# A gated mix of linear attention and a Fourier layer: the first four tiles of k' computed chunk by chunk for both column halves in eight banks, and the stores of x's rest rows moved behind the last loads of their stage

## The chip, the core and the metric

The kernel runs on one core of a Trainium2 chip. The metric is the device time of one execution in microseconds, and the figure compared is the median over several executions. A profile, taken of one more execution, records every instruction of the five engines (TensorE or PE, VectorE or DVE, ScalarE or ACT, GpSimd or POOL, SyncE or SP) and every DMA packet.

## What is computed

Two branches read the same `x` (2048 rows, 576 columns) and are mixed by a gate per row.

```
g = sigmoid(sum(x * gate_w))                          # one number per row
q, k, v = split(x @ wqkv)                             # 32 heads of 18 columns
phi(t) = where(t > 0, t + 1, exp(t)) + 1e-6
kv = phi(k)^T v;  z = sum over rows of phi(k)         # per head
a = (phi(q) kv / (phi(q) z + 1e-6)) @ wo
b = Re(DFT_seq(DFT_hidden(x)))                        # four dense DFT matrices
out = g * a + (1 - g) * b
```

All is float32. The products run on TensorE in float32r, a faster form that keeps fewer bits: an operand is split into a high part `hi` and a low part `lo = raw - hi`, and a product is `hi*hi + hi*lo + lo*hi`, three matmuls.

## The kernel before

**Stages.** In the order of time: k' = phi(x @ wk) for 16 tiles of 128 rows (lines 440 to 579, to 68 us of the profile); x^T k' for the attention's state, with one product `kv_step` per chunk of 128 columns of x (lines 582 to 690, 68 to 135 us); q' = phi(x @ wq) and the gate (from line 693, 130 to 200 us), the attention's output, and then the two DFT passes, which take the larger part of the time (lines 845 to 1205). A memory area, `arena`, is laid out by hand: names ending in `_AT` are offsets, and areas are used again from stage to stage. The framework orders instructions that touch the same bytes with semaphores.

**k'.** The contraction of 576 is cut into four chunks of 128 and a rest of 64, held as one more chunk of 128 with the rest twice (`_rows`, line 1209), so that one matmul with `hi` and one with `lo` of x do its work. The 576 columns of wk make two halves (`h`) of 288, each fitting one PSUM bank (there are eight). One half of one tile is `4 x 3 + 2 = 14` matmuls of 128x288, 28 a tile (`steps`, line 269). Tiles 4 to 15 run one after another, half by half (`k_half`, line 447). `feature` (line 338) turns a finished bank into phi: two ACT instructions (lines 340, 341) and one on DVE (342) that frees the bank; `k_split` (457) then makes the high and low parts `pk` of a whole tile. `k_split`s wait in the list `pending`.

**The first four tiles** (lines 464 to 531) go by chunks, so that matmuls can start when the first chunk of wk and x has landed: for half 0, chunk after chunk, the passes over the four tiles in four banks; then half 1 in the other four banks. `Wide.load` (294) issues the pieces of one half of wk: chunks 0, 1 and 2-3 of half 0, then the rest, then half 1 in two pieces of two chunks and its rest. Between them `load_first` (468) issues the chunks of `xf`, the first four tiles of x: chunk 0 in two parts of two tiles, chunk 1, chunks 2-3, chunk 4. Parts of `xf` go to ACT's queue, all else to SP's. As a chunk lands, ACT makes its `hi` (`hi_of`, line 172) and DVE its `lo` (`lo_of`, 182); in `Wide.split` (313) for wk, written out in the loop for x. Then come ACT's and DVE's work in the order of the program, since `pace()` (line 489) turns the framework's own ordering off for these two; SP's queue is in program order throughout. PE's order is the framework's at this stage.

**The features of the first tiles** run in two groups, half 0's four (line 525) after both halves' matmuls have been issued, then `split_next` twice (526, 527), which splits x tiles 4 and 5, then half 1's four, with two `k_split`s between them. In the loop over tiles 4 to 15 (557) each turn runs one half, splits an x tile two ahead, does a part of a `Left` (below), runs the other half and the pending `k_split`s, and issues the load of a tile four ahead (`load_next`, 253). Four slots hold tiles of x (`LAY_Q['xs']`, 78).

**DMA issue.** A DMA signals its end on one of eight semaphores in turn; the ninth DMA waits for the first one's landing, and so on.

**Left and the rest rows.** `Left` (349) prepares, beside the attention, combinations of x's transpose for the DFT stage: loads on POOL's queue, four DVE additions, `hi` and `lo`, stores. The last of them, `Left(NP)`, holds the rows left over from the contraction's 128s. It lies at `ACC_AT`, over `acc[0]` to `acc[6]`, loaded at step 6 of the second stage when k' no longer needs them there. It ends with six stores of 448 KB to `xrest` on SP's queue (lines 385 to 387), issued as soon as its parts are done, in the middle of that stage's loads: `xg_load` (539, the pieces `craw` of x), `load_pair` (600, wv and wo) . q' writes `acc` again (line 703, `feature`). `xrest` is read from line 889 on, in the DFT stage.

Of the kernel before, what the change touches and what calls it, by code (L numbers as in the profile page):

```python
# [8 lines left out]
F = mybir.dt.float32  # L9
R = mybir.dt.float32r  # L10
# [43 lines left out]
class Ring:  # L54
# [5 lines left out]
    def next(self):  # L60
        self.n += 1
        return self.at[(self.n - 1) % len(self.at)]
# [7 lines left out]
SLOT_AT, SLOT = ACC_AT + NT * D * 4 + 256, 7 * BS * P * 4  # L70
# [61 lines left out]
def kernel(  # L132
# [18 lines left out]
    nc = tc.nc  # L151
# [17 lines left out]
    def bank():  # L169
        return psum.tile([P, 512], F, tag="bank", name="bank")  # L170

    def hi_of(dst, src, bias=0.0):
        return nc.scalar.activation(dst, src, AF.Copy, bias=bias)  # L173


    pending, paced = [], ExitStack()
# [5 lines left out]
    def lo_of(dst, src, hi):  # L182
        nc.vector.tensor_tensor(out=dst, in0=src, in1=hi, op=ALU.subtract)  # L183
# [21 lines left out]
    def half(h):  # L205
        return slice(h * HALF, (h + 1) * HALF)
# [78 lines left out]
    rest_ring = Ring(CONST_AT + 3584, 1184, 2)  # L285

    class Wide:
# [6 lines left out]
        def load(self, h, pieces=(KC,), queues=None, also=lambda k: None):  # L294
# [15 lines left out]
            also(len(los))  # L310
            queues[-1].dma_start(out=rest, in_=self.src[:, KC, cols])

        def split(self, h, n=1, lo_of=lo_of):
# [12 lines left out]
            lo_of(hi[64:, KC], rest[64:], hi[64:, KC])  # L326
            yield
# [19 lines left out]
    xrest_of = xrest.rearrange("(g q j r) n -> g j r q n", g=2, q=4, j=3)  # L347

    class Left:
# [18 lines left out]
        def make(self):  # L368

            r, c = self.f[:, :, 1], self.c  # L370
            add(r[:, 0], r[:, 1], r[:, 6])
            add(r[:, 4], r[:, 2], r[:, 6], ALU.subtract)
            yield
            add(r[:, 3], r[:, 0], r[:, 2], ALU.subtract)
            add(r[:, 6], r[:, 5], r[:, 3], ALU.subtract)
            yield
            hi_of(c[:, :4, 0], r[:, :4])
            hi_of(c[:, 4:, 0], r[:, 4:])
            yield
            for fs in (slice(0, 4), slice(4, 7)):  # L380
                lo_of(c[:, fs, 1], r[:, fs], c[:, fs, 0])
                if self.k < NP:
                    nc.gpsimd.dma_start(out=xforms[self.k][:, fs], in_=c.bitcast(F)[:, fs])
                yield
            for j in range(0 if self.k < NP else 6):
                k, g = j // 2, j % 2
                nc.sync.dma_start(out=xrest_of[g, k], in_=self.plain.bitcast(F)[:, g, k // 2])

    lefts = []

    def left_part():
        while lefts:
# [50 lines left out]
    wkt = Wide(wk, dict(hi=(0, WH), lo=(2 * WH, 2 * WH + WL)), K_AT)  # L443

    done = []
# [19 lines left out]
    first, cuts = [], ((0, 1), (1, 1), (2, 2), (4, 1))  # L465
    ab = [slice(k * FT // 2 * P, (k + 1) * FT // 2 * P) for k in range(2)]

    def load_first(k):
        nonlocal first_b
        a, n = cuts[k]  # L470
        o = C_AT + a * 2 * FT * P * 4
        hi, raw, lo = (at(o + i * n * FT * P * 4, [P, n, FT * P], d, "xs")
                       for i, d in ((0, R), (1, F), (1, R)))
        src = xf[a:a + n].rearrange("c p n -> p c n")
        if k == 0:
            first_b = raw[:, :, ab[1]], src[:, :, ab[1]]
            raw_a, src = raw[:, :, ab[0]], src[:, :, ab[0]]
        elif k == 1:
# [4 lines left out]
    first_b = None  # L483
    wkt.load(0, (1, 1, 2), also=load_first)
    wkt.load(1, (2, 2))
    order += list(range(FT, NT)) + list(range(NT))
    for _ in range(3):
        load_next()
    pace()
    for h in range(2):  # L490
        ps = [bank()[:, :HALF] for _ in range(FT)]
        parts = wkt.split(h, KC)
        for c, (raw, hi, lo) in enumerate(first):
            passes = [(hi, c), (lo, c), (hi, 5 + c)][:3 if c < KC else 2]
            tiles = [range(FT)] * len(passes)
            if h == 0 and c == 0:
                a, b = ab
                nc.vector.tensor_copy(out=hi[:, a], in_=raw[:, a])
                lo_of(lo[:, a], raw[:, a], hi[:, a])
                next(parts)  # L500
                done.append(hi_of(hi[:, b], raw[:, b]))
                lo_of(lo[:, b], raw[:, b], hi[:, b])
                two = range(FT // 2), range(FT // 2, FT)
                passes = [(hi, c), (lo, c), (hi, c), (hi, 5 + c), (lo, c)]
                tiles = [two[0], two[0], two[1], range(FT), two[1]]
            elif h == 0 and c == 1:
                next(parts)
                done.append(hi_of(hi, raw))
                lo_of(lo, raw, hi)
                passes = [passes[k] for k in (0, 2, 1)]  # L510
            else:
                if h == 0:
                    done.append(hi_of(hi, raw))
                    lo_of(lo, raw, hi)
                next(parts)
            for n, (x, j) in enumerate(passes):
                for i in tiles[n]:
                    nc.tensor.matmul(ps[i], x[:, i * P:(i + 1) * P], wkt.row(h, j),  # L518
                                     start=(c == 0 and n == (0 if h or i < 2 else 2)),
                                     stop=(c == KC and n == 1))  # L520
        if h == 0:
            banks = ps
            lefts.append(Left(2, SLOT_AT + 15104, done[-1]).make())
    for i in range(FT):
        k_feature(i, 0, banks[i])
    split_next()
    split_next()
    for i in range(FT):
        k_feature(i, 1, ps[i])
        if i < 2:  # L530
            pending.pop(0)()

    WV_AT = C_AT + 4 * 2 * CU * P * 4
# [23 lines left out]
    for i in range(FT, NT):  # L557
        xs = split.pop(0)
        k_half(i, 0, xs)
        if i < NT - 2:  # L560
            split_next()
        left_part()
        if i >= NT - 2:
            xg_next()
        held = pending[:]
        pending.clear()
        k_half(i, 1, xs)
        for f in held:
            f()
        if 8 <= i < 12:  # L570
            xg_load()
        if i < NT - 1:
            load_next()
        if i == FT:
            load_next()
        for k, j in ((3, 4), (4, 9), (5, 13)):
            if i == j:
                lefts.append(Left(k, SLOT_AT + 15104 + k % 2 * 14336, done[-1]).make())
# [56 lines left out]
    for c in range(5):  # L635
        ps = [bank(), bank()]
        passes = FULL if c < KC else FULL[:2]
        for q in range(NCU):
            t = xg_split.pop(0)
            for k in range(CU):  # L640
                s = q * CU + k
                for n, (a, b) in enumerate(passes):
                    for h in range(2):
                        nc.tensor.matmul(ps[h][:, :HALF], t[:, a, k], pk[s][:, b, half(h)],  # L644
                                         start=(s == 0 and n == 0),
                                         stop=(s == NT - 1 and n == len(passes) - 1))
# [162 lines left out]
    def m_row(h, j):  # L809
        return mhi[:, j, half(h)] if j <= KC else mlo[:, j - 5, half(h)]  # L810

    wr_forms, wr_pieces = right(wr, wr_rest, ((0, T_AT + 60416), (1, T_AT + 76544),
                                              (2, T_AT + 60416)))
    xs_ring.at[3] = T_AT + 105664
# [310 lines left out]
    for i in range(NT):  # L1125
# [3 lines left out]
        for h in range(2):  # L1129
            ps = bank()  # L1130
# [164 lines left out]
```

## Time and profile before

| | |
|---|---|
| median of 3 executions | 729.3 us (728.0 to 729.98) |
| the profiled execution, its own time | 731.39 us |
| its span, first to last instruction | 729.7 us |
| DVE busy | 600.8 us (82%) |
| ACT busy | 335.4 us (46%) |
| POOL busy | 57.0 us (8%) |
| moved by DMA | 158.82 MB, mean 218 GB/s |
| share of the chain of work that ended last, PE | 96% |
| the same, DMA | 2% (line 309's wk 1.0%, wv 0.9%) |

How to read it: the span is what the trace covers, and the execution's own time adds what lies around it, 1.7 us here. "Busy" is a sum over instructions of one engine. The chain of work that ended last goes back from the last instruction to what released it, again and again, so a cause on it is one that the end of the kernel waited for. Where PE is busy without a break, the chain runs along PE. Times in the timeline are microseconds from the span's start; a row can merge several instructions of one form (x24 is 24 of them), and the bracket at its end gives the engine's idle time before the row and what ended it. In the table of stretches (windows) each engine has its busy time, then come the granted TensorE clock (1.00 is full speed), the share of time that the DMA engines worked, and GB/s.

### The profile page before, as it was taken

To read this page: it belongs to the slowest core of one execution; us is meant where nothing else is said; L and a number is where in the kernel's file an instruction comes from. 1 tells how busy PE (TensorE), PEld (TensorE's weight loads), DVE (VectorE), ACT (ScalarE), POOL (GpSimd) and SP (SyncE) were. 2 spreads that over 40 slices of the span, in tenths; PEclk is the share of its full clock that TensorE was granted. 3 is DMA by queue.
4 is the path that set the end of the run, shared out by engine and by line. 5 is a ranking of instruction groups with operands and counts; after the bars stand their busy time and mean duration, and the time that the engine had idled before them with its cause. 6 is when DMAs were issued, how large, how long until landed. Compare 5 with 4: busy or idle time off the path is not lost.

```text
span 729.7 us, 13873 instructions
## 1 busy us (share of the span) xinstructions
PE 721.5 (99%) x5444; PEld 720.0 (99%) x5444; DVE 600.8 (82%) x995; ACT 335.4 (46%) x522; POOL 57.0 (8%) x98
## 2 busy tenths in 40 slices
PE   8999999999999999999999999999999999999998
PEld 8999999999999999999999999999999999999997
DVE  4788885688999948989999989867889987788884
ACT  5898444678744544534343333322535333232231
POOL 1011210042022220000000010000000000000000
PEclk9999999999999999999999999999999999999999
DMA  7277699367558989853466576889964444444440
GB/s 254 70 247 247 249 328 340 98 189 234 189 169 295 335 304 374 279 185 119 153 217 228 186 234 210 282 282 392 391 235 146 156 150 147 152 144 157 152 152 33
DMA packets 54356, 158.82 MB, mean 218 GB/s; under 512 B 6420, under 2 KB 11092, under 8 KB 53268
## 3 DMA queue, kind: packets, MB, share of 16 engines
q1 hardware_dynamic: 45044, 118.90, 47.6%
q0 software_dynamic: 8960, 38.65, 14.4%
q8 instruction: 43, 0.70, 0.4%
q10 hardware_dynamic: 288, 0.39, 0.1%
q14 instruction: 21, 0.17, 0.1%
HBM read 115.05 MB, written 41.39 MB: 214 GB/s over the span
## 4 chain that ended last, share of the span: by engine, by line
PE 96%; DMA 2%; DVE 1%; SPq 0%; issue 0%; ACT 0%; DVEq 0%; ACTq 0%
PE bank L1067 48%; PE bank L203 23%; PE bank L912 14%; PE bank L644 7%; PE bank L518 2%; PE bank L747 1%; DMA wraw<-in_wk_dram 1%; DMA wraw<-in_wv_dram 1%; PE bank L626 1%; DVE row L1083 0%; PE bank L629 0%; DVE ys L193 0%; SPq L309 0%; ACT plain L173 0%; DVE wd L183 0%
## 5 line engine op out<-in xcount | busy, mean ns | idle before, releaser
L1067 PE MATMUL bank<-fh,c 128*128 128x288 f32 x1792 | 354.7, 294 | 0.0
L1067 PEld LDWEIGHTS bank<-fh,c 128*128 128x128 f32 x1792 | 286.7, 188 | 0.0
L1067 PE MATMUL bank<-fl,c 128*128 128x288 f32 x896 | 263.6, 294 | 0.0
L173 ACT ACTIVATE c<-craw 128x1792 fp32r<-128x1792 f32 (+1 forms) x84 | 121.5, 1448 | 187.5 <-DVE craw L193 164.6
L1067 PEld LDWEIGHTS bank<-fl,c 128*128 128x128 f32 x896 | 168.7, 188 | 0.0
L183 DVE TENSOR_TENSOR c<-craw,c 128x1792 fp32r<-128x1792 f32 (+4 forms) x86 | 142.0, 1653 | 6.6 <-ACT c L173 6.5
L193 DVE TENSOR_TENSOR craw<-craw 128x256 f32<-128x256 f32 (+1 forms) x192 | 98.3, 512 | 21.7 <-DMA craw<-in_ci_dram 11.9
L203 PE MATMUL bank<-wd,xs 128*128 128x288 f32 (+1 forms) x784 | 106.1, 296 | 0.0
L203 PEld LDWEIGHTS bank<-wd,xs 128*128 128x128 f32 x784 | 104.6, 188 | 0.1
L912 PE MATMUL bank<-wf,xf 128*128 128x288 f32 x588 | 91.1, 295 | 0.0
L912 PEld LDWEIGHTS bank<-wf,xf 128*128 128x128 f32 x588 | 83.4, 189 | 0.0
L203 PE MATMUL bank<-mw,qs 128*128 128x288 f32 x448 | 63.2, 297 | 0.0
L644 PE MATMUL bank<-pk,c 128*128 128x288 f32 x448 | 60.9, 296 | 1.1 <-DVE c L183 1.1
L644 PEld LDWEIGHTS bank<-pk,c 128*128 128x128 f32 x448 | 59.8, 189 | 1.3 <-DVE c L183 1.3
L203 PEld LDWEIGHTS bank<-mw,qs 128*128 128x128 f32 x448 | 59.9, 188 | 0.2 <-DVE qs L183 0.2
L342 DVE SCALAR_TENSOR_TENSOR acc<-bank,e 128x288 f32<-128x288 f32 x64 | 28.4, 454 | 17.7 <-ACT e L341 17.6
L193 DVE TENSOR_TENSOR ys<-bank,ys 128x288 f32<-128x288 f32 x63 | 28.8, 457 | 16.4 <-PE bank L1067 13.4
L183 DVE TENSOR_TENSOR fl<-fl,fh 128x864 fp32r<-128x864 f32 (+1 forms) x32 | 34.7, 1093 | 6.5 <-ACT fh L173 5.3
L173 ACT ACTIVATE fh<-fl 128x864 fp32r<-128x864 f32 (+1 forms) x32 | 29.8, 949 | 16.6 <-DVE fl L193 16.6
L912 PE MATMUL bank<-wf,xr 96*128 96x288 f32 x112 | 33.3, 298 | 0.0
L1132 ACT ACTIVATE acc<-bank,gate 128x288 f32<-128x288 f32 x32 | 16.0, 501 | 35.1 <-PE bank L203 34.8
L193 DVE TENSOR_TENSOR ys<-ys,bank 128x288 f32<-128x288 f32 x47 | 21.2, 450 | 13.0 <-PE bank L1067 12.4
(107 smaller groups left out, 668.0 us busy)
## 6 DMA issues: line engine op xcount, KB each, us to landing
xf<-xm SPq DMA_DIRECT2D x42, 512.0 KB, 6.7
craw<-in_cr_dram SPq DMA_DIRECT2D x32, 512.0 KB, 4.1
craw<-in_ci_dram SPq DMA_DIRECT2D x32, 512.0 KB, 3.5
xraw<-in_xa_dram SPq DMA_DIRECT2D x28, 320.0 KB, 3.0
xm<-xb POOLq DMA_DIRECT2D x8, 1024.0 KB, 6.6
wf<-wm SPq DMA_DIRECT2D x14, 576.0 KB, 5.9
xr<-xr SPq DMA_DIRECT2D x14, 448.0 KB, 8.8
xm<-xb POOLq DMA_DIRECT2D x8, 768.0 KB, 6.2
```

The source lines that it names most:

```text
L173: return nc.scalar.activation(dst, src, AF.Copy, bias=bias)
L183: nc.vector.tensor_tensor(out=dst, in0=src, in1=hi, op=ALU.subtract)
L193: nc.vector.tensor_tensor(out=dst, in0=a, in1=b, op=op)
L203: nc.tensor.matmul(ps, a, b, start=(n == 0), stop=(n == len(pairs) - 1))
L342: nc.vector.scalar_tensor_tensor(dst, ps, 0.0, e, op0=ALU.max, op1=ALU.add)
L518: nc.tensor.matmul(ps[i], x[:, i * P:(i + 1) * P], wkt.row(h, j), start=(c == 0 and n == (0 if h or i < 2 else 2)), stop=(c == KC and n == 1))
L626: nc.tensor.matmul(kv_of(g), wvt[c][:, 0, gs], gts[c][:, :, gs], start=(c == 0 and g % 2 == 0), stop=(c == 4), skip_group_check=True)
L644: nc.tensor.matmul(ps[h][:, :HALF], t[:, a, k], pk[s][:, b, half(h)], start=(s == 0 and n == 0), stop=(s == NT - 1 and n == len(passes) - 1))
L747: nc.tensor.transpose(banks[c // KC][:, (c % KC) * P:(c % KC + 1) * P], a, ident)
L912: nc.tensor.matmul(ps, a, b, start=(start and n == 0), stop=(n == len(ops) - 1), skip_group_check=True)
L1067: nc.tensor.matmul(ps[q], c[x][:, l, k], factors[p](y, f), start=(p == 0 and i == 0), stop=(p == NP - 1 and i == 2))
L1132: done.append(nc.scalar.activation(acc[i][:, half(h)], ps[:, :HALF], AF.Copy, scale=gate[:, i:i + 1]))
```

## The change

1. **Loads.** A new `load_both` issues both halves of wk, chunk by chunk: chunk 0 of half 0, of half 1, chunk 1 of both, chunks 2-3 of both, then the rests. The second part of chunk 0 of `xf` goes out right behind the first piece of wk, chunk 1 of `xf` as before on ACT's queue, chunks 2-3 behind four pieces of wk, chunk 4 behind six.
2. **Order of the matmuls.** Eight banks are taken at once. For each chunk 0 to 3 both halves' passes run, 24 matmuls of four tiles; the rest chunk runs tile by tile, two matmuls for half 0 and two for half 1, so that tile 0's banks are finished first. The number of matmuls stays 112.
3. **Splits and features.** ACT and DVE split x and wk in that order, then three tiles of x (4, 5, 6), and then all eight features run in a row, tile by tile, with one `k_split`. The loop over tiles 4 to 15 splits no tile in its first turn and runs at most two pending `k_split`s a turn. Four loads of x tiles are issued ahead instead of three, and one load in the loop's first turn is gone.
4. **Rest rows.** `Left` keeps its tile in `rest_stores`; `store_rest()` issues the six stores just ahead of q's first `load_next`, that is on SP's queue behind the last `craw`, wv and wo loads of the second stage.

```diff
+        def load_both(self, pieces, also):
...
+            c = 0
+            for i, k in enumerate(pieces):
+                for h in range(2):
+                    o = lo + h * steps[0] + c * n * 4
+                    raw = at(o, [P, k, n], F, "wraw")
+                    got[h][1].append((c, at(o, [P, k, n], R, "wd"), raw))
+                    if h == 0 and i:
+                        also(i)
+                    nc.sync.dma_start(out=raw, in_=self.src[:, c:c + k, half(h)])
+                    if h == i == 0:
+                        also(0)
+                c += k
+            also(len(pieces))
+            for h in range(2):
+                nc.sync.dma_start(out=got[h][2], in_=self.src[:, KC, half(h)])
+                self.got[h] = got[h]
...
-            for j in range(0 if self.k < NP else 6):
-                k, g = j // 2, j % 2
-                nc.sync.dma_start(out=xrest_of[g, k], in_=self.plain.bitcast(F)[:, g, k // 2])
-
-    lefts = []
+            if self.k == NP:
+                rest_stores.append(self.plain.bitcast(F))
+
+    lefts, rest_stores = [], []
+
+    def store_rest():
+        t = rest_stores.pop()
+        for k in range(3):
+            for g in range(2):
+                nc.sync.dma_start(out=xrest_of[g, k], in_=t[:, g, k // 2])
...
-    wkt.load(0, (1, 1, 2), also=load_first)
-    wkt.load(1, (2, 2))
+    wkt.load_both((1, 1, 2), load_first)
     order += list(range(FT, NT)) + list(range(NT))
-    for _ in range(3):
+    for _ in range(4):
         load_next()
     pace()
...
+    ps = [[bank()[:, :HALF] for _ in range(2)] for _ in range(FT)]
+    parts = [wkt.split(h, KC) for h in range(2)]
...
+    for c, (raw, hi, lo) in enumerate(first):
+        if c == 0:
+            a, b = ab
+            nc.vector.tensor_copy(out=hi[:, a], in_=raw[:, a])
+            lo_of(lo[:, a], raw[:, a], hi[:, a])
+            next(parts[0])
+            done.append(hi_of(hi[:, b], raw[:, b]))
+            lo_of(lo[:, b], raw[:, b], hi[:, b])
+            next(parts[1])
+        else:
+            if c == 1:
+                next(parts[0])
+            done.append(hi_of(hi, raw))
+            lo_of(lo, raw, hi)
+            if c > 1:
+                next(parts[0])
+            next(parts[1])
+        if c == KC:
+            break
+        for h in range(2):
+            passes = [(0, hi, c), (1, lo, c), (2, hi, 5 + c)]
+            tiles = [range(FT)] * 3
...
+            for (n, x, j), those in zip(passes, tiles):
+                for i in those:
+                    first_step(i, h, x, c, n, j)
+    lefts.append(Left(2, SLOT_AT + 15104, done[-1]).make())
+    for _ in range(3):
+        split_next()
     for i in range(FT):
-        k_feature(i, 0, banks[i])
-    split_next()
-    split_next()
+        for h in range(2):
+            for n, x in enumerate((hi, lo)):
+                first_step(i, h, x, KC, n, KC)
     for i in range(FT):
-        k_feature(i, 1, ps[i])
-        if i < 2:
+        for h in range(2):
+            k_feature(i, h, ps[i][h])
+        if i > 2:
             pending.pop(0)()
...
     for i in range(FT, NT):
         xs = split.pop(0)
         k_half(i, 0, xs)
-        if i < NT - 2:
+        if FT < i < NT - 2:
             split_next()
...
-        held = pending[:]
-        pending.clear()
+        held = pending[:2]
+        del pending[:2]
...
         if i < NT - 1:
-            load_next()
-        if i == FT:
             load_next()
...
+    store_rest()
     wr_forms, wr_pieces = right(wr, wr_rest, ((0, T_AT + 60416), (1, T_AT + 76544),
                                               (2, T_AT + 60416)))
     xs_ring.at[3] = T_AT + 105664
     load_next()
```

More of the change, by code (lines that the diff above doesn't have):

```diff
@@ L311, in load @@
             queues[-1].dma_start(out=rest, in_=self.src[:, KC, cols])
+        def load_both(self, pieces, also):
+            n = HALF
+            lo, hi = self.start + self.lay["lo"][0], self.start + self.lay["hi"][0]
+            steps = [self.lay[k][1] - self.lay[k][0] for k in ("lo", "hi")]
+            rests = [rest_ring.next() for _ in range(2)]
+            got = [[at(hi + h * steps[1], [P, 5, n], R, "wd"), [],
+                    at(rests[h], [P, n], F, "wraw")] for h in range(2)]
+            c = 0
[14 more added lines that the diff above has]
+                self.got[h] = got[h]
         def split(self, h, n=1, lo_of=lo_of):
@@ L468, in load_first @@
     def load_first(k):
-        nonlocal first_b
         a, n = cuts[k]
@@ L477, in load_first @@
             raw_a, src = raw[:, :, ab[0]], src[:, :, ab[0]]
-        elif k == 1:
             nc.sync.dma_start(out=first_b[0], in_=first_b[1])
@@ L481, in load_first @@
         first.extend((raw[:, i], hi[:, i], lo[:, i]) for i in range(n))
-    first_b = None
-    wkt.load(0, (1, 1, 2), also=load_first)
-    wkt.load(1, (2, 2))
+    wkt.load_both((1, 1, 2), load_first)
     order += list(range(FT, NT)) + list(range(NT))
-    for _ in range(3):
+    for _ in range(4):
         load_next()
     pace()
[L490 to L502, printed above, removed]
+    ps = [[bank()[:, :HALF] for _ in range(2)] for _ in range(FT)]
@@ new lines, with first_step @@
+    parts = [wkt.split(h, KC) for h in range(2)]
+    def first_step(i, h, x, c, n, j):
+        nc.tensor.matmul(ps[i][h], x[:, i * P:(i + 1) * P], wkt.row(h, j),
+                         start=(c == 0 and n == 0), stop=(c == KC and n == 1))
+    for c, (raw, hi, lo) in enumerate(first):
[20 more added lines that the diff above has]
+            tiles = [range(FT)] * 3
+            if c + h == 0:
@@ L503 @@
                 two = range(FT // 2), range(FT // 2, FT)
-                passes = [(hi, c), (lo, c), (hi, c), (hi, 5 + c), (lo, c)]
+                passes = [passes[k] for k in (0, 1, 0, 2, 1)]
                 tiles = [two[0], two[0], two[1], range(FT), two[1]]
[L506 to L509, printed above, removed]
+            elif h == 0:
                 passes = [passes[k] for k in (0, 2, 1)]
[L511 to L523, printed above, removed]
+            for (n, x, j), those in zip(passes, tiles):
+                for i in those:
+                    first_step(i, h, x, c, n, j)
```

## The prediction

> **What bounds the kernel now.** I read the page's head first, then the stretches, the chain of waits, and the timeline where PE stops.
>
> ```profile
> span 729.7 us, 13873 instructions
> PE 721.5 (99%) x5444; PEld 720.0 (99%) x5444; DVE 600.8 (82%) x995; ACT 335.4 (46%) x522; POOL 57.0 (8%) x98
> ```
>
> PE is out of work for 729.7 − 721.5 = 8.2 us in all, so nothing but TensorE's gaps and its clock can pay. The table of stretches (columns: PE, PEld, DVE, ACT, POOL busy with counts; clock; DMA share; GB/s) says where they lie:
>
> ```profile
> 0.80:4.50 3.70, 3.30 (x17) 3.30 (x17) 0.32 (x2) 2.04 (x3) 1.39 (x6) 1.00 0.71 213
> 4.50:8.31 3.81, 3.81 (x27) 3.29 (x25) 2.35 (x5) 1.39 (x3) 0.00 (x0) 1.00 0.93 318
> 8.31:10.22 1.91, 0.00 (x0) 0.00 (x0) 0.59 (x1) 1.07 (x2) 0.00 (x0) 1.00 1.07 388
> 11.10:14.60 3.50, 3.50 (x17) 3.50 (x16) 2.93 (x7) 2.18 (x6) 1.62 (x2) 0.51 0.88 326
> 124.60:128.70 4.10, 2.68 (x20) 2.21 (x18) 2.31 (x5) 3.23 (x7) 0.00 (x0) 1.00 0.86 271
> ```
>
> Three losses are in the change's reach: 1.91 us without a matmul before 10.22, a stretch of about 3.5 us at half the clock right behind it, and 4.10 − 2.68 = 1.42 us around 126. The DMA engines are full during the first (share 1.07) and fetch more than the matmuls next in line need. The chain of waits agrees:
>
> ```profile
> 2.67 7.04 DMA wraw<-in_wk_dram
> 9.73 0.45 ACT wd L173
> 10.22 13.45 PE bank L518 x88
> 23.67 44.55 PE bank L203 x336
> 68.22 19.18 PE bank L644 x144
> ```
>
> The last row gives the undisturbed price of one 128x288 matmul: 19.18 / 144 = 0.1332 us. The 88 from 10.22 on would take 11.72, and took 13.45: 1.73 lost to the clock, which fits half of 3.5.
>
> **Part 1, the chunk order.** What PE starts on, and what it waits for:
>
> ```profile
> 3.90 0.29 DVE L498 CAST xs<-xs 128x256 fp32r<-128x256 f32 x1 [3.90 <-DMA xs<-in_xf_dram]
> 4.50 3.81 PE L518 MATMUL bank<-wd,xs 128*128 128x288 f32 x24
> 5.42 0.45 ACT L173 ACTIVATE wd<-wraw 128x288 fp32r<-128x288 f32 x1
> 8.97 0.63 ACT L173 ACTIVATE xs<-xs 128x512 fp32r<-128x512 f32 x1 [2.58 <-DMA xs<-in_xf_dram]
> 9.73 0.44 ACT L173 ACTIVATE wd<-wraw 128x288 fp32r<-128x288 f32 x1
> ```
>
> Chunks 0 and 1 of half 0 are 24 matmuls, 3.20 us of work; they took 3.81, so 0.61 is small waits for splits. Then chunk 2's x (landed 8.97) and wk (9.73) are awaited. In the new order chunks 0 and 1 are 48 matmuls: 4.50 + 0.61 + 48 x 0.1332 = 11.50 before chunk 2 is asked for. The third piece on SP's queue, which was ready for ACT at 5.42, is now wk's chunk 0 for half 1, and PE wants it at 4.50 + 0.61 + 1.60 = 6.7.
>
> Two more pieces of wk (128 x 288 x 4 bytes = 0.147 MB each) now go ahead of chunk 2. At the 388 GB/s of the gap that is 0.76 us: x at 9.73, wk at 10.49, its `hi` done 0.44 later and PE free to go at 10.98, 0.5 us **before** it is wanted. The second half's piece, 0.295 MB, follows at 11.25 and its `lo` by 12.2; PE wants it at 11.50 + 1.60 = 13.1. wk's chunks 2-3 must wait for the first DMA to land (3.90, by the eight semaphores), long before their turn in a full queue. Bounds for chunk 2: 0.5 us earlier if transfers keep strictly to the order of issue, 1 us later (11.5 to 12) if small rows are slower than the mean. I take 10.98.
>
> From 11.50 the other 64 matmuls take 8.53: PE is done with the four tiles at 20.03 instead of 23.67, **3.64 us earlier** (= 1.91 + 1.73: the matmuls stay 112). This supposes that without the gap the half clock goes too. The Trainium skill, "TensorE: Matmul & The Clock Gate", section "Part 1: The HAM clock gate (the "warmup" mystery)", lets the clock fall only after at least one idle window of about 3.4 us; by that a gap of 1.91 is too short and the gain would be 1.91. The row at 11.10 stands against it: 0.51 begins 0.9 us after the only gap there is. It stays a rival below.
>
> **Part 1, what comes behind.** All eight features now stand in a row, behind three splits of x. In the trace:
>
> ```profile
> 16.95 0.41 ACT L340 ACTIVATE e<-bank 128x288 f32<-128x288 f32 x1 [1.15 <-PE bank L518]
> 17.75 0.39 ACT L340 ACTIVATE e<-bank 128x288 f32<-128x288 f32 x1
> 17.88 0.46 DVE L342 SCALAR_TENSOR_TENSOR acc<-bank,e 128x288 f32<-128x288 f32 x1 [1.43 <-ACT e L341]
> 18.52 0.39 ACT L340 ACTIVATE e<-bank 128x288 f32<-128x288 f32 x1
> 20.07 1.35 ACT L173 ACTIVATE xs<-xraw 128x640 fp32r<-128x640 f32 x2
> 31.02 1.24 ACT L173 ACTIVATE pk<-acc 128x576 fp32r<-128x576 f32 x2
> 36.33 1.92 ACT L173 ACTIVATE xb<-xb 128x1024 fp32r<-128x1024 f32 x2
> 40.28 0.72 ACT L173 ACTIVATE xs<-xraw 128x640 fp32r<-128x640 f32 x1
> 41.03 0.83 DVE L183 TENSOR_TENSOR xs<-xraw,xs 128x640 fp32r<-128x640 f32 x1 [0.17 <-ACT xs L173]
> ```
>
> A feature costs ACT 0.77 (18.52 − 17.75), up to 0.86 alone. The splits are done before tile 0 is: their data came in the same place of the queue before, and before 20.07 ACT split nothing because features stood ahead. Banks: tile 0's first bank is finished 14 matmuls (1.86 us) ahead of the last, a feature takes 1.39 (16.95 to 17.88 + 0.46), so tile 4 starts without a wait. But the queue behind is long. Counted from PE's start on tile 4, ACT begins the first feature at −1.65 and has, up to the split of tile 9, 15 features (x 0.80 = 12.0), six `pk` (x 0.65 = 3.9), three splits (2.16) and `Left`'s two (1.92): 20.0 in all, to 18.35, and DVE's `lo` to 19.2. PE wants it after 140 matmuls and two more, 18.9. Before, it was ready at 41.86 and wanted at 23.67 + 18.9 = 42.6. Late by 0 to 1.2 (features at 0.77 or 0.86); I take **0.3**. The next split has slack again, as a turn gives ACT about 3.5 us of work and lasts 3.7.
>
> **Part 2, the rest rows.**
>
> ```profile
> 112.48 6.00 SPq L387 DMA_DIRECT2D xr<-xb  x6
> 118.59 1.04 SPq L544 DMA_DIRECT2D craw<-in_xg_dram  x1
> 119.73 0.82 SPq L605 DMA_DIRECT2D wraw<-in_wv_dram  x1
> 122.88 7.54 SPq L605 DMA_DIRECT2D wraw<-in_wo_dram  x5
> 125.94 2.38 PE L644 MATMUL bank<-pk,c 128*128 128x288 f32 x16 [1.07 <-DVE c L183]
> 128.67 0.38 PE L626 MATMUL bank<-gt,plain 128*126 128x252 f32 x1 [0.35 <-DVE gt L183]
> 135.27 3.75 PE L203 MATMUL bank<-wd,xs 128*128 128x288 f32 x27
> 137.48 0.46 DVE L342 SCALAR_TENSOR_TENSOR acc<-bank,e 128x288 f32<-128x288 f32 x1
> 144.64 0.82 DVE L183 TENSOR_TENSOR xs<-xraw,xs 128x640 fp32r<-128x640 f32 x1
> xr<-xb SPq DMA_DIRECT2D x6, 448.0 KB, 5.0
> ```
>
> The six stores hold SP for 6 us and the DMA engines for 2.7 MB; `craw` and wv behind them come late, and PE waits 1.07 and 0.35 us. With the stores gone the loads go out up to 6 us earlier, and both waits go: **1.42 us**. Bounds: 1.0 if one of the loads is bound by its slot, 1.42 at most.
>
> What is added: the stores now follow wo's last issue, at 122.88 + 7.54 − 4.8 (the sum below) = 125.6. They take 6 us to issue and 5 to land, so the last lands by 136.6, sooner if the queue is empty. They read `ACC_AT`, which q's first feature overwrites, and DVE would write there at 137.48 − 4.8 = 132.7. So a **new wait** of up to 4 us stands on DVE, in order before everything else of q'. Who waits behind it: five banks can still be filled (three hold kv), 70 matmuls or 9.3 us from 129.9 on, so no bank is missed before 139. Next PE needs the `lo` of q's tile 3, done at 144.64 + 0.82, which in the new time is 140.7; it is wanted only after tiles 0 to 2 and the last `kv_step`, 135.27 − 4.8 + 77 x 0.1332 + 1.1 (an estimate for the ten matmuls of one `kv_step`, of the kind of 128.67's row) = 141.8. Behind the wait DVE has some 4 us of its own up to that `lo`, so a landing up to 137 costs nothing, and each us later costs one. q's loads of x behind the stores on SP's queue wait for 135.27's end in any case. I take 0. PE has no other cover to lose here: q tile 0's matmuls stand between the state's end and the last `kv_step`.
>
> **Sum.** 3.64 − 0.3 + 1.42 = 4.8 us. The profiled execution took 731.39 (span 729.7), so 726.6; the median shown is 2.1 lower, 729.3, and the same sum from there gives **724.5**. All stages from 140 us on are PE without a gap and move along.
>
> **Rivals.** Two stretches and the page's clock line (40 slices, 9 is 0.9 or more) bear on them:
>
> ```profile
> 23.67:42.30 18.63, 18.63 (x143) 18.63 (x142) 13.94 (x26) 17.17 (x38) 1.45 (x2) 1.00 0.36 114
> 128.70:140.00 11.30, 11.30 (x89) 11.30 (x90) 7.04 (x16) 7.31 (x18) 0.00 (x0) 1.00 0.30 90
> ```
>
> ```profile
> PEclk9999999999999999999999999999999999999999
> ```
>
> *The half clock isn't the gap's.* It began 0.9 us after work had resumed, so it could come at a set time of the run; and the executions spread over 1.98 us (728.0 to 729.98) with the profile 2.1 above the median, as if some had no such stretch to lose. Then 1.73 is not won: 724.5 + 1.7 = 726.2. Against it: the page's clock line has no slice under 0.9, so nothing like it comes again, and no other gap before the end is as long. The rule of the Trainium skill's page "TensorE: Matmul & The Clock Gate" named above leads here too.
>
> *Chunk 2 still comes late.* With wk's chunk at 12 instead of 10.49 PE waits 1 us, and the clock falls behind the gap as before: 1.0 + 1.7, so 727.2. For it: 0.5 us of slack on a transfer that ends after 10. Against: a gap of 1 would be half the one seen, and might leave the clock alone.
>
> *The gain is hidden anyway*, or the order takes no hold: ACT's queue stays behind for several tiles and eats the 3.6 won. For it: ACT is busy for 17.17 of 18.63 us there. Against: PE waits for ACT nowhere in it. Price 1.2 per tile, for three tiles: 728.
>
> *Slower: the new wait on DVE.* If the six stores land late, q's first feature, and all DVE work behind it, hold PE. It decides from a landing at 137; at 142.5 it has eaten the whole gain, and with the stores at half speed behind wo and x it could reach 144: 731. For it: an in-order engine and no cover of its own. Against: the DMA share is 0.3 in that time.
>
> **How the numbers follow.** Forecast 0.52, half clock 0.20, chunk 2 late 0.14, hidden 0.07, slower 0.07. A difference under 0.3% (2.2 us, below 727.1 is faster) can't be told from no change. Faster: 0.52 + 0.19 and a third of chunk 2 late, 0.75; slower: 0.06; the rest 0.19. The range: 1.7 below the forecast (the small waits of 0.61, no lateness on ACT, and the spread), up to 728.2, over the first three cases: 722.8 to 728.2, leaving out the last two and tails.
>
> **What would show it.** Right: the four tiles' 112 matmuls in one row from 4.5 to 20, no row near 0.5 in the clock before 20, tile 4 at 20; between 112 and 126 no `xr` issue and no PE idle time; the first q feature on DVE idle for 2 to 4 us "from DMA xr", PE busy through it. Wrong: PE idle before a chunk 2 matmul, a wait for `xs` at tile 9 over 1 us, or PE idle between 135 and 145.

## The result and the profile after

The changed kernel took 727.88 us (median of 22 executions, 726.43 to 730.03) against 729.11 (22, 728.00 to 731.51) of the kernel before: ratio 0.9981, 95% interval 0.9972 to 0.9989. That is 1.4 us faster by the ratio, where 4.8 were forecast. It is less than the 2.2 us that the prediction called the least that can be told from no change; with 22 executions of each kernel the interval still leaves out 1. The profiled execution took 726.95.

The head of the page, then from TensorE's timeline, the chain and the waits of the changed kernel (waits: us in total, times, longest):

```profile
span 725.2 us, 13882 instructions
PE 720.0 (99%) x5444; PEld 718.8 (99%) x5444; DVE 600.5 (83%) x995; ACT 335.7 (46%) x522; POOL 57.1 (8%) x98
```

```profile
4.64 15.22 PE L520 MATMUL bank<-wd,xs 128*128 128x288 f32 x112
```

```profile
19.86 44.59 PE bank L203 x336
```

```profile
PE bank L229 <- POOL ones_f L225: 1.2, 1, 1.2
PE bank L1100 <- DVE c L183: 0.3, 1, 0.3
```

The four tiles' 112 matmuls are one row without a gap, tile 4 starts at 19.86 instead of 23.67, and its stage runs at 44.59 / 336 = 0.1327 us a matmul, so nothing waits for a split at tile 9. The rest-row stores, in the queue of SP and on DVE, and two stretches (columns as in the prediction):

```profile
119.70 6.18 SPq L637 DMA_DIRECT2D wraw<-in_wo_dram  x5
126.06 5.91 SPq L419 DMA_DIRECT2D xr<-xb  x6
```

```profile
137.19 0.82 DVE L367 SCALAR_TENSOR_TENSOR acc<-bank,e 128x288 f32<-128x288 f32 x2 [5.72 <-ACT e L366]
```

```profile
120.00:125.00 5.00, 5.00 (x42) 5.00 (x41) 2.07 (x5) 1.75 (x4) 0.00 (x0) 1.00 0.69 216
125.00:130.00 5.00, 5.00 (x39) 5.00 (x39) 2.93 (x5) 3.39 (x9) 0.00 (x0) 1.00 0.79 288
```

The loads of wo go out at 119.70 instead of 122.88, the stores behind them, and PE is busy for all ten us around the old waits. DVE stands idle for 5.72 us before q's first feature (the trace names ACT as the releaser, but by ACT's timeline that feature's `e` was done at 131.69 + 0.45; so I take 137.2 for the landing of the stores, which is inferred; the six stores, issued from 126.06 on, took 5.8 us from issue to landing in the median).

From profile to profile the span fell by 729.7 − 725.2 = 4.5 us, almost the 4.8 of the sum. From median to median the time fell by 1.2. The two profiled executions make up the difference of 3.2: the one before lies 2.28 above its kernel's median of 729.11, the one after 0.93 below its own. So the steps fit the execution that they were read from, and the question is what that execution had that others have not.

### The profile page after: what moved, and what is told of

It is laid out like the page before. It is cut to its first block, busy times and chain, and to the rows that moved or that the text cites. A ratio compares the mean times of both kernels' runs of the same rounds, so it can differ in the third digit from the quotient of the medians.

```text
span 725.2 us, 13882 instructions
## 1 busy us (share of the span) xinstructions
PE 720.0 (99%) x5444; PEld 718.8 (99%) x5444; DVE 600.5 (83%) x995; ACT 335.7 (46%) x522; POOL 57.1 (8%) x98
## 4 chain that ended last, share of the span: by engine, by line
PE 93%; DMA 3%; DVE 2%; issue 1%; POOL 0%; ACT 0%; SPq 0%; DVEq 0%; ACTq 0%; POOLq 0%
PE bank L1100 48%; PE bank L203 23%; PE bank L945 14%; PE bank L676 3%; PE bank L520 2%; PE bank L779 1%; DMA craw<-in_xg_dram 1%; DMA wraw<-in_wv_dram 1%; DMA xm<-xb 1%; DVE ys L193 1%; PE bank L229 1%; POOL xb L389 0%; PE bank L658 0%; DVE c L183 0%; ACT xb L173 0%
```

## The experiments

The theory was that the first profile was an unusual execution: the cost of its late chunk 2 isn't there in a typical one. The rival: the order is worth 3.64 us in each execution and something, the stores first of all, gives it back. The first four ran side by side: each half of the change alone, and both kernels once more for a second profile.

**1. The order alone** (the stores issued in `Left.make` as before).

```diff
-            if self.k == NP:
-                rest_stores.append(self.plain.bitcast(F))
+            for j in range(0 if self.k < NP else 6):
+                k, g = j // 2, j % 2
+                nc.sync.dma_start(out=xrest_of[g, k], in_=self.plain.bitcast(F)[:, g, k // 2])
...
-    store_rest()
```

> The new chunk order and features, with the rest-row stores left where they were. Theory A (the profiled execution of before was an unusually slow one: the median one has a shorter gap before chunk 2 or no half clock, so the order is worth much less than the 3.64 us that the profile shows): 0 to 1 us faster than before in the median, 0.9985 to 1.0. Theory B (the order is worth its 3.64 us in every execution and the moved stores give most of it back in executions that were not profiled): 3 to 4 us faster, 0.995 to 0.996.

Measured: 0.9988 [0.9976, 1.0000], 728.50 against 729.16, as theory A has it; theory B's 0.995 to 0.996 lie outside the interval.

**2. The stores alone** (the kernel before, with `rest_stores` and `store_rest` of the change).

> Only the rest-row stores are moved; the start is that of before. Theory A: faster by the 1.42 us of the two waits around 126 us, ratio about 0.998, the profile without PE idle time there and with DVE idle ahead of q's first feature. Theory B: slower by about 2 us, 1.003, with PE idle between 135 and 145 us.

Measured: 1.0001 [0.9990, 1.0011]. No gain at all, which neither theory has.

**3 and 4. Both kernels again, unchanged.**

> The kernel before once more, for a second profile of it. Theory A: the gap before chunk 2 is clearly shorter than 1.91 us, or no stretch of half clock follows, and the span is 726 to 728 us instead of 729.7. Theory B: gap and half clock are there again as in the first profile, within 0.3 us. Ratio 1.000 by both.

> The changed kernel once more, for a second profile of it. Theory A: the start is as in its first profile (112 matmuls without a gap, done at about 19.7 us), the span 725 to 727. Theory B: a new PE idle time of 1 to 3 us shows between 135 and 145 us. Ratio to before 0.998 by both.

Measured: 1.0002 [0.9993, 1.0012] and 0.9978 [0.9968, 0.9989].

The second profile of the kernel before settles the first question. Mean clock, first and second profile:

```profile
core 0: 729.7 us, clock 0.997
```

```profile
core 0: 726.9 us, clock 1.000
```

TensorE's first matmuls, chunk 2's split on ACT, and the chain in that second profile:

```profile
4.64 16.45 PE L518 MATMUL bank<-wd,xs 128*128 128x288 f32 x112
```

```profile
7.91 0.63 ACT L173 ACTIVATE xs<-xs 128x512 fp32r<-128x512 f32 x1 [1.34 <-DMA xs<-in_xf_dram]
```

```profile
21.09 44.55 PE bank L203 x336
```

Chunk 2's x is there at 7.91, not 8.97; the 112 matmuls are one row (a gap would part it), 16.45 long with 16.45 − 112 x 0.1332 = 1.5 of small waits, and there is no half clock. Tile 4 starts at 21.09. The order is worth 16.45 − 15.22 = 1.2 us here, not 3.64. The eight other profiles of the old order without added copies do have a gap ahead of chunk 2, but one of 0.27 to 0.95 us, and the 88 matmuls behind it then take 11.92 to 11.94 us, at full clock. In that of experiment 2:

```profile
9.10 11.93 PE L523 MATMUL bank<-wd,xs 128*128 128x288 f32 x88 [0.34 <-ACT wd L173]
```

And how rare the first case is: a stretch of 3.4 us at half the clock costs the mean 1.7 / 727 = 0.0023 of 1, so it shows as 0.998 or less. Of the 96 executions of the kernel before that stood beside experiments 1 to 12 with a clock recorded, none has that; of the 12 of experiment 3, one.

The second profile of the changed kernel misses what was expected of it (span 728.2 instead of 725 to 727, tile 4 at 20.57), and shows what the order is good for:

```profile
8.92 0.63 ACT L173 ACTIVATE xs<-xs 128x512 fp32r<-128x512 f32 x1 [0.75 <-DMA xs<-in_xf_dram]
```

```profile
4.64 15.93 PE L520 MATMUL bank<-wd,xs 128*128 128x288 f32 x112
```

Chunk 2's x is as late here as in the first profile (8.92 beside 8.97), yet there is no gap and no half clock: tile 4 starts 0.71 us later than in the first profile of this kernel, where in the old order the late chunk went with a start 2.56 us above the mean of the others. That is one execution of each.

That explains the order. It doesn't explain why the stores' half gave nothing, since its profile has the wait of 1.42 us gone. Here is what TensorE waited for in the profile of experiment 2, and in that of 4:

```profile
PE bank L649 <- ACT c L173: 1.5, 1, 1.5
```

```profile
PE bank L676 <- ACT c L173: 1.1, 1, 1.1
```

A wait at 105 to 113, for a piece `craw` of x, stands where the two profiles of the kernel before list none. In experiment 4 the piece's split on ACT, SP's queue, and what SP waited for:

```profile
109.19 0.63 ACT L173 ACTIVATE c<-craw 128x512 fp32r<-128x512 f32 x1 [5.80 <-DMA craw<-in_xg_dram]
```

```profile
98.06 0.38 SPq L309 DMA_DIRECT2D wraw<-in_wq_dram  x1
98.48 1.69 SPq L311 DMA_DIRECT2D wraw<-in_wq_dram  x1
100.69 1.06 SPq L578 DMA_DIRECT2D craw<-in_xg_dram  x1
```

```profile
SPq L309 <- DMA xm<-xb: 3.0, 3, 2.4
```

q's first weight load waits on SP for a store of POOL's (`xm`), and the piece of x of the same step is queued behind it. That gave two questions: does the gap itself call the half clock (5, 6, 12), and are the two waits, the early one for `craw` and the late one of the stores, in each other's place (7 to 11)?

**5 and 6. A gap in every execution.** ACT copies chunk 2's x some times more, in the kernel before (5) and the changed one (6):

```diff
+                    for _ in range(3 if c == 2 else 0):
+                        hi_of(hi, raw)
                     done.append(hi_of(hi, raw))
...
+            for _ in range(7 if c == 2 else 0):
+                hi_of(hi, raw)
             done.append(hi_of(hi, raw))
```

> The kernel before with three more copies of chunk 2's x on ScalarE ahead of the one that TensorE waits for: 3 x 0.64 us (0.64 is the copy's duration in every profile) puts a gap of about 2 us ahead of chunk 2 into every execution, as the first profile had it by a late transfer (1.92 us, then 0.5 clock for 3.4 us). Theory A (the gap itself calls the half clock, so what the first profile showed is one case that a late transfer makes): the first 88 matmuls after the gap show a stretch at 0.5, tile 4 starts near 24.5 instead of 21.1, and the time is 3.4 to 3.7 us above the kernel before, ratio about 1.005. Rival (the half clock of the first profile had another cause, and a gap costs only itself): no stretch under 0.99, tile 4 near 23.0, +1.9 us, ratio about 1.0026.

> The changed kernel with seven more copies of chunk 2's x on ScalarE ahead of the one that TensorE waits for: 7 x 0.64 = 4.5 us, of which the 48 matmuls now ahead of chunk 2 hide all but about 2.2 us. Here the gap comes after 6.4 us of work instead of 3.8. Theory A (a gap of 2 us in the first 15 us calls the half clock): a stretch at 0.5, tile 4 near 23.8 instead of 19.86, time 3.5 to 4 us above the changed kernel. Rival (the gap costs only itself): clock 1.0 throughout, tile 4 near 22.1, +2.2 us. If e5 shows the half clock and this one not, the work ahead of the gap decides.

Measured: 5 at 1.0026 [1.0014, 1.0038], 6 at 1.0011 [0.9999, 1.0023], by the ratios 2.3 us above the changed kernel (0.9978 to 0.9981). Stretches of 5, the gap and what follows, and then of 6:

```profile
8.61:11.34 2.73, 0.01 (x2) 0.00 (x1) 0.35 (x1) 2.58 (x5) 0.00 (x0) 1.00 1.07 402
12.40:15.80 3.40, 3.40 (x17) 3.40 (x17) 2.83 (x6) 2.21 (x6) 1.62 (x2) 0.54 0.45 160
```

```profile
11.60:13.72 2.12, 0.00 (x2) 0.00 (x1) 0.35 (x1) 2.06 (x5) 0.00 (x0) 1.00 0.79 314
13.72:18.00 4.28, 4.28 (x32) 4.28 (x33) 4.22 (x10) 4.19 (x10) 1.62 (x2) 1.00 0.10 14
```

A gap made on purpose brings the half clock in the profile of 5, but only 3 of its 9 executions have a mean of 0.998 or less, so the median pays for the gap alone: its profile is theory A's, its ratio exactly the rival's 1.0026. In 6 it is one of 10. Neither theory holds as it stood: a gap of 2 to 3 us **can** call the half clock and often doesn't.

**12. A gap at the first profile's place, in the new order** (five more copies of chunk 1's x).

> The changed kernel with five more copies of chunk 1's x on ScalarE: 3.2 us, so that a gap of about 2 us comes after the first 24 matmuls (near 8.2), at the place and with the length that the first profile had (1.92), with the order of the changed kernel. In e5 a gap of 2.72 at 8.6 was followed by clock 0.5, in e6 one of 2.12 at 11.6 was not. Theory (the place decides: a gap of 2 us that begins about 3.5 us after the first matmul calls the half clock): 0.5 for some 3 us from about 11 to 14, tile 4 near 23.6, time 3.7 us above the changed kernel. Rival (the length decides, about 2.1 is too short as a rule, and the first profile's case was a chance of phase): clock 1.0, tile 4 near 21.9, +2.0 us.

Measured: 1.0011 [1.0000, 1.0022], 730.38, as 6 some 2.3 us above the changed kernel. The gap came out shorter than meant, in TensorE's timeline:

```profile
4.64 4.18 PE L520 MATMUL bank<-wd,xs 128*128 128x288 f32 x24
10.33 11.95 PE L520 MATMUL bank<-wd,xs 128*128 128x288 f32 x88 [1.51 <-ACT xs L173]
```

Here the profile has full clock, and three of the 10 executions have 0.997 or 0.998; of the 34 of the changed kernel without added copies, one. Place and length aren't told apart by it.

**7 and 11. The two weight loads of q one step later**, behind the pieces of x; the changed kernel otherwise.

```diff
-            if step in (8, 11):
-                wqt.load(step == 8)
+            if step in (9, 12):
+                wqt.load(step == 9)
```

> The changed kernel with q's two weight loads put one step later in the kv stage (steps 9 and 12 instead of 8 and 11), so that they stand behind the pieces of x of steps 9 and 12 in SP's queue. The first load waits 2.3 us on SP for POOL's store in the profile after, and the piece of step 9 waits with it. Theory (the waits for craw at 105 to 113, 0.13, 1.08 and 1.67 us in the three profiles with the stores moved, come from that queue): those waits are gone, the kernel is 0.5 to 1 us faster than the changed one, ratio to before about 0.997. Rival (the spread of single transfers makes them, whatever the order): the waits stay in the same range and the time is that of the changed kernel, 0.998.

> The kernel of e7 once more, since that had only five executions: Theory A: ratio 0.9965 to 0.9975, about 1 us below the changed kernel (0.998), no wait from 95 to 130. Rival (e7's few executions were the good end of the changed kernel's): ratio 0.998, and a wait of 0.5 us or more at 105 to 113.

Measured: 0.9967 [0.9954, 0.9980] (5 executions) and 0.9968 [0.9956, 0.9980] (12): 726.85 against 729.14, **faster than the kernel before in both**, and by the ratios 0.8 to 1.0 us under the changed kernel, as the theory has it. The two were not run side by side, and the intervals overlap a little. In the profile of 7 SP issues the load later, without a wait, and the piece is split 3.8 us earlier than in 4 (0.5 of it because tile 4 started that much earlier):

```profile
100.09 0.39 SPq L309 DMA_DIRECT2D wraw<-in_wq_dram  x1
```

```profile
105.37 0.64 ACT L173 ACTIVATE c<-craw 128x512 fp32r<-128x512 f32 x1 [2.90 <-DMA craw<-in_xg_dram]
```

```profile
105.00:110.00 5.00, 5.00 (x40) 5.00 (x39) 4.12 (x8) 2.98 (x6) 0.00 (x0) 1.00 0.77 261
```

TensorE has no wait from 95 to 130 in either profile.

**9. The stores' half with the loads one step later**, k' in its old order, and **10. the loads alone**, on the kernel before.

> The kernel before with the stores moved and q's two weight loads one step later, k' in its old order. Theory A (the stores' half removes 0.6 to 1.4 us at 120 to 130, and waits for craw at 105 to 113, 1.67 and 1.23 us in the two profiles of that half alone, give it back; both gone, the gain stays): no wait of TensorE from 95 to 130, ratio 0.998 to 0.9985. Rival (the stores' half is worth 0.3 us whatever stands beside it): ratio 0.9995 and waits as before.

> The kernel before with q's two weight loads one step later and nothing else; the stores stay where they block SP. Theory A (the two waits stand in series, and the one of the stores stays): 0.5 to 1.5 us of waiting at 115 to 130, none at 105 to 113, ratio 0.999 to 1.0005. Rival (the loads alone make the gain of e7 against the changed kernel, about 1 us): ratio 0.9985.

Measured: 9 at 0.9975 [0.9965, 0.9985], 727.22, without a wait from 95 to 130. That is 1.9 us, more than theory A's 1.1 to 1.5, where the stores' half alone gave 0 to 0.7. The waits that go make up about 1.0 of the 1.9 (the table below). Some 0.7 more lie in waits too short for the idle column. Here are 105 to 110 us in the second profile of the kernel before, which has no early wait in the table, and in that of 9:

```profile
105.00:110.00 5.00, 5.00 (x37) 4.64 (x36) 2.84 (x5) 1.38 (x3) 0.00 (x0) 1.00 0.91 298
105.00:110.00 5.00, 5.00 (x40) 5.00 (x39) 4.49 (x9) 1.92 (x4) 0.00 (x0) 1.00 0.91 315
```

Both count as busy throughout, but three matmuls fewer, 0.40 us, got done in the first. From tile 4's start to the first DFT pass 9 takes 241.91 us, the kernel before 243.62 in the mean (last column of the table), so 1.7 of the 1.9 lie there. 10 at 1.0049 [1.0034, 1.0064], 733.17: outside both expectations. Its SP queue, its wait, and the stretches behind it:

```profile
109.89 5.94 SPq L387 DMA_DIRECT2D xr<-xb  x6
115.94 0.98 SPq L309 DMA_DIRECT2D wraw<-in_wq_dram  x1
118.42 0.38 SPq L544 DMA_DIRECT2D craw<-in_xg_dram  x1
```

```profile
PE bank L644 <- DVE c L183: 2.7, 1, 2.7
```

```profile
122.33:124.98 2.65, 0.00 (x1) 0.00 (x1) 0.42 (x1) 0.96 (x2) 0.00 (x0) 1.00 0.96 326
125.90:129.20 3.30, 3.30 (x18) 3.30 (x17) 2.96 (x7) 2.51 (x7) 0.00 (x0) 0.56 0.66 182
```

The second weight load, which had gone out ahead of the six stores, now stands behind them and in front of the pieces of x that follow. The late wait grows to 2.65, and the half clock comes after it, 100 us into work without a long gap: 9 of the 10 executions have 0.998 or less (where in the nine that were not profiled isn't shown). So the loads one step later cost 3.6 us with the stores in their old place and gain with the stores moved: it is the stores' move that lets the loads be moved.

**8, 13 to 16. Is the early wait a chance?** The stores' half again (8), and two more profiles each of it and of the kernel before, unchanged.

> The stores' half of the change alone, once more (1.0001 [0.999, 1.0011] the first time, against a wait of 0.58 to 1.42 us that it removes at 120 to 130). Theory A (the half is worth under 0.6 us in a typical execution because waits for craw at 105 to 113 take its place): ratio 0.9995 to 1.0, and this profile has no wait at 120 to 130 but 0.5 to 1.7 us at 105 to 113. Rival (the first comparison was low by chance, the half is worth the 1 us that e4 against e1 shows): ratio 0.9985 to 0.999, no wait at either place.

> The kernel before, a third profile. So far the two have no wait of TensorE at 105 to 115 and 1.42 and 0.58 us at 118 to 130. Theory A (the early wait for craw is a chance of the transfers, alike wherever the stores stand): an early wait of about 1 us is as likely here as with the stores moved, and where it comes the late one is small. Rival B (the early wait comes with the moved stores): none at 105 to 115, 0.5 to 1.5 us at 118 to 130. Both: tile 4 starts at 21.0 to 21.4.

> The stores' half alone, a third profile. So far 1.55 and 1.23 us of waiting for craw at 105 to 115 and none at 118 to 130. Theory A: 0 to 1.6 us, without a rule. Rival B: over 1 us again. Both: none at 118 to 130, tile 4 at 21.0 to 21.4.

> The kernel before, a fourth profile; as for the third: theory A an early wait as likely as not, rival B none at 105 to 115 and 0.5 to 1.5 us at 118 to 130.

> The stores' half alone, a fourth profile; as for the third: theory A 0 to 1.6 us at 105 to 115, rival B over 1 us; both none at 118 to 130.

Measured: 8 at 0.9990 [0.9981, 0.9999]; 13 and 15 at 728.27 and 728.39, 14 and 16 at 728.24 and 727.82, one execution each. By its ratio 8 falls to the rival, by its profile (1.23 us of early wait, no late one) to theory A. The waits for `craw` in the fourth profile of the kernel before (15), and in 16:

```profile
PE bank L644 <- ACT c L173: 0.9, 1, 0.9
```

```profile
PE bank L649 <- ACT c L173: 0.2, 1, 0.2
```

TensorE's idle time in all profiles of kernels that don't change ACT's work, but for 10, from stretches like those above (early: 103 to 116.5; late: 116.5 to 131). The last column is the time from tile 4's start to the first DFT pass by the chain (in 9: 21.13 to 263.04), which holds the waits too short for the idle columns as well:

| stores | profile | early | late | sum | tile 4 to DFT |
|---|---|---|---|---|---|
| old place | before | 0 | 1.42 | 1.42 | 243.96 |
| | 3 | 0 | 0.58 | 0.58 | 243.29 |
| | 13 | 0.62 | 0 | 0.62 | 243.31 |
| | 15 | 0.92 | 0 | 0.92 | 243.40 |
| | 1 | 0.51 | 0.86 | 1.37 | 244.12 |
| moved | after | 0.13 | 0 | 0.13 | 242.67 |
| | 2 | 1.66 | 0 | 1.66 | 244.34 |
| | 8 | 1.23 | 0 | 1.23 | 243.72 |
| | 14 | 0.14 | 0 | 0.14 | 242.59 |
| | 16 | 0.20 | 0 | 0.20 | 242.65 |
| | 4 | 1.08 | 0 | 1.08 | 243.57 |
| moved, loads later | 7 | 0 | 0 | 0 | 241.97 |
| | 9 | 0 | 0 | 0 | 241.91 |
| | 11 | 0 | 0 | 0 | 242.05 |

The late wait is away in each profile with the stores moved. The early one comes and goes: rival B (none with the stores in their old place, over 1 us with them moved) fails on 13 and 15 and on 14 and 16, and theory A stands, though so few profiles can't rule out that the move makes the early wait somewhat longer. Where it is 0.6 or more in the old place there is no late one; a TensorE that has lost that time may find the late pieces there already, which is argued and not shown. Means with the stores in their old place and moved: 0.98 and 0.74 of idle time, 243.62 and 243.26 in the last column. The stores' half is worth 0.24 or 0.36 us by them, not 1.42, and beside the spread of the rows it can't be told from nothing. The loads one step later give 1.28 us on top (243.26 to 241.98), in each of three profiles.

## Why the prediction was wrong

- **Where the losses lie**: right for that execution. Only TensorE's gaps and clock counted, and the stages from 140 us on moved along with the start, but for single waits in the DFT passes, 0.5 to 1.0 us in 1, 4, 7 and 10. Three of these four have the new order; whether that is chance isn't shown.
- **"3.64 us earlier (= 1.91 + 1.73)"**: this is the step that failed, by its size. Gap and half clock go, as forecast, and from the first profile to the one after it was 3.81 (23.67 to 19.86). But tile 4 starts, in the nine other profiles of the old order without added copies, at 21.09, 21.03, 21.32, 21.13, 21.12, 21.20, 21.16, 21.17 and 20.79, mean 21.11; in the five of the new order at 19.86, 19.84, 20.57, 20.05 and 20.43, mean 20.15. A typical execution wins **0.96 us**. The rest was one late transfer and its consequence: of the 2.56 us by which the first profile's tile 4 lies above that mean, 1.03 come from the row of 88 matmuls starting at 10.22 instead of 9.19 (the mean of the eight others with such a row) and 1.52 from its taking 13.45 instead of 11.93. So the half clock cost 1.5, not 1.73: at full clock the row takes 11.93 and not the 11.72 of the sum.
- **The time of chunk 2**: x was forecast at 9.73, and split from 7.86 in the profile after, with two more pieces ahead of it. The order has more room than forecast, since the landing that it was counted from was the late one.
- **ACT late by 0.3 at tile 9**: 0.
- **"1.42 us" for the stores**: a second term mis-sized. Both waits go, as said; worth about 0.24 to 0.36, because the wait for `craw`, which no row of the first profile shows, takes the place of it, and because other profiles of the kernel before have 0.58 to 1.37 in the place of 1.42. Experiment 9 takes both waits away and gains 1.9, 10 takes the early one alone and the late one grows to 2.65: they are in series.
- **The new wait on DVE**: there, 5.72 us against "up to 4", the landing at 137.2 against 136.6, and no cost to TensorE, as forecast. The slower case did not come.
- **Sum and base**: 0.96 + 0.24 to 0.36 = 1.2 to 1.3 us by the profiles, beside 1.2 of the medians and 1.4 to 1.6 of the two ratios; the closeness owes something to luck, as the second term is smaller than its spread. The sum of one slow execution was taken off the median of others: with the profile at 731.39 and all three runs at 729.98 or less, 2.1 us of the loss may not be in the median to be won. The text saw this ("as if some had no such stretch to lose") and used it for a rival only. That 727.88 lies in the stated range, near its upper end, is due to the rivals that the range was drawn over.
- **The rival on the half clock**: its time, 726.2, is nearer, but its reason isn't shown: experiments 5 and 10 call the half clock by a gap. Chunk 2 was not late. The rival that the gain is hidden comes nearest with 728, by luck: its reason, an ACT queue behind for several tiles, did not occur.
- **The clock line of the page**, read as "nothing like it comes again", can't show that: a slice is 729.7 / 40 = 18.2 us, and 3.4 us at half the clock leave 1 − 1.7 / 18.2 = 0.91 of it, a 9. The pages of 5 and 10 have the same line, word for word. It is the mean clock of 0.997 that leaves room for one such stretch and not for two.
- **A slip in a rival's sum**: with 137 as the last landing that costs nothing and a price of one us each, the whole 4.8 is eaten at 141.8, not 142.5.

## What to carry to other kernels

Before a gap in a profile is priced, compare that execution with the other runs: what it lies above them may not be there to be won in the median, and a second profile of the same kernel tells which rows are chance. A wait that is removed is worth only what no wait ahead of it or behind it in the same queue then takes; test it together with the neighbour. Idle time in a table of stretches leaves out short waits; the time between two fixed points of the program has them. Here the loads of the next stage, moved one step behind the pieces that TensorE needs first, gave another 0.8 to 1.0 us on top of the change, and on the kernel before the same move cost 3.6.

## What was not expected of the hardware

- Half the clock after gaps of 1.92, 2.72 and 2.65 us: each was followed by about 3.4 us at 0.50, from 11.2, 12.7 and 125.4 us on, which is 0.4 to 1.4 us after work had resumed; 2.12 and 1.51 us in profiles of 6 and 12 were not, and the same kernel shows it in some executions only. The Trainium skill, "TensorE: Matmul & The Clock Gate", section "Part 1: The HAM clock gate (the "warmup" mystery)", says that the monitor's window of about 3.4 us runs freely, and asks for one whole idle window. A free-running window would fit that the delay differs and that the same gap sometimes costs double; that a whole idle window is needed does not fit the rows here. What decides between two gaps of the same length stays open.
- The landing of a transfer as a source of spread: without added copies, chunk 2's x was split from 7.62 to 8.13 us on in nine profiles with the old order and from 8.97 in one, and from 7.55 to 8.25 in four with the new order and from 8.92 in one. In the first profile's landing records 15 of the 16 DMA engines had it by 7.58 and the last at 8.94, in the late one of the new order 15 by 7.69 and the last at 8.89; why that one was late isn't shown.
